# Loading tap 0's weights between the two halves of the samples, and splitting its products at output 254

## The chip, the cores and the metric

The kernel runs on one core of one Trainium2 chip. The metric is the device time of one execution in microseconds (us). An execution is also taken by the hardware profiler; its page, its groups of instructions, its waits, its timeline and its chain of work are the "profile" of this text. Engines: PE multiplies matrices (PEld is its weight load), DVE and ACT work on vectors and read PSUM, POOL is the general engine, SP issues the DMAs.

## The reference

Two convolutions of five taps over time, each followed by gelu and by taking every second output, then a joint network: every time step is added to every one of 8 label vectors, tanh, and a last matrix.

```python
B, T, D, K, U = 2, 4000, 512, 5, 8
h = sum over i of einsum("btc,cd->btd", xp[:, i:i+T], w1[i])   # xp: x padded by 2 on both sides
h = gelu(h)[:, ::2]                                             # 2000 steps
f = sum over i of einsum("btc,cd->btd", hp[:, i:i+T1], w2[i])
f = gelu(f)[:, ::2]                                             # 1000 steps
j = tanh((f @ w_f)[:, :, None, :] + (g @ w_g)[:, None, :, :])
return einsum("btud,dv->btuv", j, w_o)
```

Everything is bf16; the result is 2 x 1000 x 8 x 512.

## The kernel before

Channels lie on the 128 partitions in NK = 4 blocks, time along the free dimension. The kernel is a list of operations (`Plan`, L75 to L345): each names its engine, what it reads and writes and an assumed cost. `schedule` (L171) orders the operations of PE, ACT, DVE and POOL by these costs, except those that are pinned to the written order (`pl.pin`); `emit` puts a semaphore wait in front of an instruction whose input comes from another engine or from a DMA. All loads are pinned, so SP issues them in the order in which the code names them. In PSUM the unit of a wait is one of 8 banks; in SBUF it is a cell of 4 bytes.

**First convolution.** The first batch's outputs 0 to ND - 1 (ND = 444) are computed directly: five taps, each of them four column blocks m, each the sum of four products of 128 x 128 weights with ND columns, 80 products in all (`direct`, L750). Their input is `eo`: the samples, turned so that channels are on the partitions, even samples in eo[0] and odd ones in eo[1]. Taps 0, 4 and 2 read even samples, taps 1 and 3 odd ones (`TAPS` = 0, 4, 2, 1, 3).

The samples come by two plain loads of 512 samples each into xr[0] and xr[1] (`load_xr`, L508; "first" and "second" samples below), are turned on PE by products with the identity (L582) into PSUM, and copied from there into `eo` by DVE (L592) and ACT (L480). One copy takes all four channel blocks of every fourth sample; DVE takes one of the two residues r and ACT the other, so their outputs alternate column by column in `eo`:

```python
lo = 16 + 2 * P * rt + r
o = eo[pp, :, lo:lo + 2 * P - 1:2]
```

Two neighbouring bf16 columns share a cell of 4 bytes, so ACT's copy waits for DVE's.

**Order of the loads.** First samples, second samples, tap 0, then the taps 4, 2, 1 and 3 with transposing loads of x into `xa` between them (L520 to L542). A load of a tap waits until the load three places before it has landed (`came[-3]`). Seven products of zeros (`warm_mm`) run before the samples are there, and two more after the first eight turns.

**The other outputs.** The rest of the first convolution is computed in triples (`Triple`, L635): three neighbouring outputs from nine products, instead of fifteen, on sums and differences of samples (`xa`, `xp`, `row`) and of weights (`w1_t`, `w1_x`). The first batch's outputs behind ND are NF = 184 triples on `xa` and NL = 336 on `xp[1]`; the second batch has two lots of 334. DVE and ACT make the sums of weights (`w1part`, L616; wu, ws, wv, ssum are its intermediate tiles) and of samples (`Triple.step`, L651) while PE works on the direct outputs. The weight work begins with taps 0 and 4 and goes on with tap 2. Each unit (one triple lot and one column block m) takes two banks in turn, from the lists `even` and `odd` (L633). The direct outputs use the banks 4, 6, 0 and 2.

**Behind it** come the second convolution, also in triples, and the joint network: tanh on ACT, the last product in a scheme of seven products instead of eight, whose sums POOL makes, and stores of 128 x 512 tiles.

Of the kernel before, what the change touches and what calls it, by code (L numbers as in the profile page):

```python
# [7 lines left out]
ACT = mybir.ActivationFunctionType  # L8
# [4 lines left out]
P = 128  # L13
# [341 lines left out]
def bass_standalone__seq2seq_rnn_t_joint__speech_kernel(  # L355
# [22 lines left out]
    NK = D // P  # L378
    assert (B, T, D, K, U) == (2, 4000, 512, 5, 8)
    T1, T2 = T // 2, T // 4  # L380
    NT3 = (T2 + 2) // 3
    ND, NF = 444, 184
    NL = 2 * NT3 - ND // 3 - NF
    assert ND % 6 == 0 and NF % 2 == 0 and NL % 2 == 0
    EW = 16 + 4 * P
# [5 lines left out]
    NT = 512  # L391
    NWARM = 7
    TAPS = (0, 4, 2, 1, 3)
    NX = 2

    with ExitStack() as es:
        cur = [16512]

        def at(name, shape, dtype, offset=None):
            o = cur[0] if offset is None else offset  # L400
            b = Buf(nc, name, shape, dtype, o)
            if offset is None:
                cur[0] = (b.end + 31) // 32 * 32
            return b
# [3 lines left out]
        w1_sb = at("w1_sb", [K, NK, D], BF16)  # L408
# [9 lines left out]
        xr = [Buf(nc, f"xr{i}", [4, NK, P], BF16, h_off + 16384 + i * 4096) for i in range(NX)]  # L418
# [10 lines left out]
        ident = at("ident", [P], BF16)  # L429
# [3 lines left out]
        eo = Buf(nc, "eo", [2, NK, EW], BF16, w2_sb.end - w2_sb.bytes)  # L433
# [40 lines left out]
        def tt(eng, o, a, b, op):  # L474
            pl.op(eng, lambda e: e.tensor_tensor(out=o.ap, in0=a.ap, in1=b.ap, op=op), (a, b), (o,),  # L475
                  0.02 + 2.14e-3 * o.ap.free_size() if eng == "pool" else vec_cost(o, (a, b)))

        def act(o, i, func, scale=1.0, bias=None):
            rd = (i,) if bias is None else (i, bias)
            pl.op("act", lambda e: e.activation(o.ap, i.ap, func, scale=scale,  # L480
                                                bias=0.0 if bias is None else bias.ap), rd, (o,),
                  o.ap.free_size() * 0.833e-3 + (0.05 if i.psum else 0.105 if bias is None else 0.186))

        def mm(o, pairs, start, stop, check=True):

            def fn(e):
                for n, (l, r) in enumerate(pairs):
                    ins = e.matmul(o.ap, lhsT=l.ap, rhs=r.ap, start=start and n == 0,  # L488
                                   stop=stop and n == len(pairs) - 1, skip_group_check=not check)
                return ins  # L490
            pl.op("pe", fn, [v for pr in pairs for v in pr], (o,), len(pairs) * max(o.ap.free_size() / 2400 + 0.0028, 0.056))
# [7 lines left out]
            out=idv.ap, in_=zero[0:P].ap, compare_op=ALU.not_equal, fill=1.0, base=0,  # L499
# [5 lines left out]
        def load_w(eng, dst, src, slack=0.0):  # L505
            return pl.dma(eng, lambda e: e.dma_start(dst.ap, src), (), (dst,), slack=slack)

        def load_xr(rt):  # L508
            dst = xr[rt][:].map(lambda a: a.rearrange("p r k c -> p (r k c)"))
            src = x[0, 4 * P * rt:4 * P * (rt + 1), :].rearrange("(p r) c -> p (r c)", r=4)  # L510
            return pl.dma("sp", lambda e: e.dma_start(dst.ap, src), (), (dst,), rate=370e3)
# [50 lines left out]
        for ph in (4, 0, 2, 1, 3, 5):  # L562
            load_x6(xp[2], 1, ph, 0, 16)

        def warm_mm(lo, hi):
            z, zz = zero[0:P], zero[:]
            for i in range(lo, hi):
                mm(ps.cols((2 * i + 1) % 8 * NT, NT), [(z, zz)], True, True)
                pl.ops[-1].cost = 0.43

        warm_mm(0, NWARM)
        psb = ps.h[:, :].bitcast(BF16)
        for pp in range(2):
            for rt in range(NX):
                for r in range(2):
                    bk = 2 * rt if pp else 4 * rt + 2 * r
                    lo = bk * 1024 + pp * r * 512
                    pv = View(psb[:, lo:lo + 512].rearrange("p (k c) -> p k c", k=NK), np.array([bk]), True)

                    def fn(e, rt=rt, pp=pp, r=r, pv=pv):  # L580
                        for k in range(NK):
                            ins = e.transpose(pv.ap[:, k, :], xr[rt].h[:, 2 * r + pp, k, :], ident.h[:, :])  # L582
                        return ins
                    pl.op("pe", fn, (xr[rt][:], ident[:]), (pv,), 0.22 if pp and rt else 0.43)
                    if not pp and not rt and r:
                        warm_mm(NWARM, NWARM + 2)
                    lo = 16 + 2 * P * rt + r
                    o = eo[pp, :, lo:lo + 2 * P - 1:2]
                    if r:
                        act(o, pv, ACT.Copy)  # L590
                    else:
                        pl.op("dve", lambda e, o=o, pv=pv: e.tensor_copy(out=o.ap, in_=pv.ap), (pv,), (o,), vec_cost(o, (pv,)))  # L592

        def stt(eng, o, a, f, b):
            pl.op(eng, lambda e: e.scalar_tensor_tensor(  # L595
                out=o.ap, in0=a.ap, scalar=f, in1=b.ap, op0=ALU.mult, op1=add), (a, b), (o,),
                  vec_cost(o, (a, b), False))
# [32 lines left out]
                tt("dve", w1_t[1, :, sl], w(1), w(3), add)  # L630
                act(w1_t[0, :, sl], w(1), ACT.Copy, scale=2.0)

        even, odd = [4, 6, 0, 2], [1, 3, 5, 7]  # L633

        class Triple:  # L635

# [38 lines left out]
            def product(self, which, m, bank, start):  # L675
                at_z, i = self.HOME[which]
                w, p = self.w[which]
                n = self.n
                mm(ps.cols(bank * NT, n),
                   [(w[p, k, m * P:(m + 1) * P],  # L680
                     self.z_[i, k, self.off:self.off + n] if at_z else self.r_[i, k, 0:n]) for k in range(NK)],
                   start, True, False)


        class Unit:
# [13 lines left out]
                return ps.cols(self.B * NT, self.t.n)  # L699

            def s1(self):
                self.A = even.pop(0)
# [8 lines left out]
            def s3(self):  # L711
                self.t.product("t1", self.m, self.A, False)
                self.t.product("s1", self.m, self.A, False)
                self.B = odd.pop(0)
                stt("dve", self.pb(), self.pa(), 0.5, self.c)
                tt("dve", self.v, self.pb(), self.s, add)
                self.t.out(1, self.m, self.v)

            def s4(self):
                self.t.product("t0", self.m, self.A, False)  # L720
                self.t.product("s0", self.m, self.A, False)
                self.t.out(0, self.m, self.pa())
                even.append(self.A)

            def s5(self):
                self.t.product("ti", self.m, self.B, False)
                self.t.product("si", self.m, self.B, False)
                self.t.out(2, self.m, self.pb())
                odd.append(self.B)

        def to_h(b, j0, n=NT3):
            def out(r, m, src):
# [26 lines left out]

        pl.pin = False  # L760
        h_edges(0)
        for i in TAPS:
            direct(i)
        for m in range(NK):
            v = ps.cols((4 + 2 * m) % 8 * NT, ND).map(lambda a: a.rearrange("p (q r) -> p r q", r=6))
            act(hT[0][:, m, HOFF:HOFF + ND // 6], v, ACT.Gelu_apprx_tanh)
        for m in range(NK):
            w1part(m, "04")
# [12 lines left out]
                load_w("sp", v[:], src.rearrange("(k c) d -> c k d", c=P))  # L781

        def bank():
            even.append(even.pop(0))
            return even[-1] * NT

        def ge():
            c0 = bank()
# [107 lines left out]
                sems[key] = [nc.alloc_semaphore(f"s_o{len(sems)}"), 0]  # L896
            return sems[key]

        even += odd
        odd = free = even  # L900
        H = NT // 2

        def take():
# [263 lines left out]
```

## Time and profile before

| | us |
|---|---|
| median of 3 runs (lowest, highest) | 255.1 (254.69, 255.27) |
| the profiled execution | 254.9 |
| its span, first to last instruction | 253.1 |
| PE busy, of the span | 246.5 |
| DVE busy, ACT busy | 210.4, 210.6 |
| direct products: first at, first triple product at | 7.76, 23.99 |
| mean granted clock of PE | 1.00 |

The page gives the busy time of each engine and the chain of work that ended last, followed back from the last instruction. A busy engine does not have to be the one that sets the end, so it is read together with busy time by stretch, with the chain in order of time, and with the timeline, in which the brackets at a line's end name the idle time before an instruction and what ended it. Durations of PE in the timeline hold the way through the array, so the distance of one start from the next is the cost of a product in a row of them.

### The profile page before, as it was taken

Reading aid. Unit: us, or ns where it says so; the run is one execution under the profiler, and the core shown is the slowest. Engines: PE = TensorE matmul, PEld = TensorE weight load, DVE = VectorE, ACT = ScalarE, POOL = GpSimd, SP = SyncE. Lnnn points to the kernel's source line nnn. Section 1 sums busy time; section 2 is a strip of 40 time slices with the busy share of each in tenths; the row PEclk is TensorE's granted clock in tenths of the full one; section 3 lists DMA queues with packets and bytes.
Section 4 is the critical chain, followed back from the end, with each engine's and each line's share of the span. In section 5 each row is a group of like instructions: output and inputs, shape, how many; then the busy total and the mean of one; then the engine's idle time right before and its main releaser. Section 6 shows DMA issues by size and latency. Waiting matters only on the chain.

```text
span 253.1 us, 5249 instructions
## 1 busy us (share of the span) xinstructions
PE 246.5 (97%) x1899; PEld 180.1 (71%) x1905; DVE 210.4 (83%) x342; ACT 210.6 (83%) x352; POOL 103.1 (41%) x107
## 2 busy tenths in 40 slices
PE   8799999999999999999999999999999999999994
PEld 3355977666666666667458878877778888787882
DVE  2799999955999999196446799799899999999783
ACT  3497989759958866984699999999999999998762
POOL 1000000000000000001518899698998999998500
PEclk9999999999999999999999999999999999999999
DMA  6999999989000034000001322332344446555646
GB/s 246 281 238 189 202 174 185 136 201 322 3 0 0 3 104 148 0 1 3 0 0 64 104 84 85 130 123 85 105 148 143 138 143 203 166 166 171 205 134 222
DMA packets 55159, 31.99 MB, mean 126 GB/s; under 512 B 32062, under 2 KB 54878, under 8 KB 55134
## 3 DMA queue, kind: packets, MB, share of 16 engines
q1 hardware_dynamic: 54846, 31.47, 46.7%
q8 instruction: 15, 0.25, 0.4%
q10 hardware_dynamic: 288, 0.20, 0.3%
q14 instruction: 10, 0.08, 0.1%
HBM read 7.86 MB, written 16.38 MB: 96 GB/s over the span
## 4 chain that ended last, share of the span: by engine, by line
PE 85%; DVE 8%; DMA 3%; issue 2%; ACT 0%; DVEq 0%
PE acc L488 85%; DMA w_sb<-in_w_dram 2%; DVE wu L595 2%; DVE row L475 2%; DMA xr<-in_x_dram 1%; DVE xa L475 1%; DVE ssum L475 1%; DVE w_t L475 1%; DVE og L475 1%; DVE ws L475 0%; DVE w_x L475 0%; DVE sd L475 0%; DVE wv L475 0%; DVE eo L592 0%; DVE acc L595 0%
## 5 line engine op out<-in xcount | busy, mean ns | idle before, releaser
L475 DVE TENSOR_TENSOR og<-acc,sn 128x512 bf16<-128x512 f32 x84 | 55.6, 683 | 6.4 <-PE acc L488 4.4
L480 ACT ACTIVATE jT<-feT,geT 128x1000 bf16<-128x1000 f32 (+6 forms) x56 | 52.6, 1013 | 0.5 <-DVE feT L802 0.4
L488 PE MATMUL acc<-tw,ss 128*128 128x256 f16 x336 | 46.0, 273 | 0.0
L488 PE MATMUL acc<-row,w_sb 128*128 128x334 bf16 (+2 forms) x224 | 38.9, 296 | 0.0
L488 PEld LDWEIGHTS acc<-tw,ss 128*128 128x128 f16 x336 | 32.6, 98 | 7.7 <-ACT sn L909 0.4
L909 ACT ACTIVATE sn<-acc 128x512 f32<-128x512 f32 x54 | 34.6, 654 | 3.8 <-PE acc L488 3.5
L972 POOL TENSOR_TENSOR ss<-jT 128x512 f16<-128x512 bf16 x23 | 28.8, 1263 | 13.4 <-ACT jT L480 10.8
L488 PE MATMUL acc<-wo_sb,jT 128*128 128x256 bf16 (+1 forms) x187 | 31.5, 292 | 0.3
L488 PEld LDWEIGHTS acc<-row,w_sb 128*128 128x128 bf16 x224 | 21.0, 97 | 8.8 <-DVE sd L475 0.2
L472 POOL MEMSET hT<- 128x8 bf16 (+2 forms) x6 | 0.8, 148 | 63.0 <-ACT hT L480 46.3
L480 ACT ACTIVATE jX<-feT,geT 128x1000 bf16<-128x1000 f32 (+4 forms) x28 | 26.2, 983 | 0.0
L480 ACT ACTIVATE hT<-acc 128x334 bf16<-128x334 f32 (+3 forms) x36 | 15.4, 436 | 10.4 <-PE acc L488 9.9
L595 DVE SCALAR_TENSOR_TENSOR acc<-acc,sd 128x334 f32<-128x334 f32 (+2 forms) x24 | 11.6, 485 | 14.4 <-PE acc L488 14.0
L488 PEld LDWEIGHTS acc<-wo_sb,jT 128*128 128x128 bf16 x192 | 18.7, 98 | 6.2
L910 DVE COPY sn<-acc 128x512 f32<-128x512 f32 x30 | 20.5, 685 | 2.5 <-PE acc L488 2.4
L480 ACT ACTIVATE sd<-acc 128x334 f32<-128x334 f32 (+2 forms) x48 | 20.0, 434 | 2.8 <-PE acc L488 1.9
L475 DVE TENSOR_TENSOR row<-row 128x1336 bf16<-128x1336 bf16 (+2 forms) x24 | 19.1, 798 | 0.0
L972 POOL TENSOR_TENSOR ss<-jX 128x512 f16<-128x512 bf16 x15 | 17.4, 1169 | 1.1 <-ACT jX L480 0.6
L488 PE MATMUL acc<-xp,w_t 128*128 128x334 bf16 (+1 forms) x96 | 17.6, 305 | 0.0
L488 PE MATMUL acc<-hT,w_t 128*128 128x334 bf16 x96 | 17.6, 304 | 0.0
L488 PE MATMUL acc<-xp,w_x 128*128 128x334 bf16 (+1 forms) x96 | 17.1, 305 | 0.0
L488 PE MATMUL acc<-eo,w_sb 128*128 128x444 bf16 x80 | 15.6, 351 | 1.4 <-DMA w_sb<-in_w_dram 1.4
(111 smaller groups left out, 513.3 us busy)
## 6 DMA issues: line engine op xcount, KB each, us to landing
out_dram<-og SPq DMA_DIRECT2D x98, 128.0 KB, 2.0
w_sb<-in_w_dram SPq DMA_DIRECT2D x10, 512.0 KB, 5.3
out_dram<-ost SPq DMA_DIRECT2D x10, 128.0 KB, 1.9
xr<-in_x_dram SPq DMA_DIRECT2D x2, 512.0 KB, 3.8
wf_sb<-in_w_f_dram SPq DMA_DIRECT2D x1, 512.0 KB, 3.7
wg_sb<-in_w_g_dram SPq DMA_DIRECT2D x1, 512.0 KB, 4.8
wo_sb<-in_w_o_dram SPq DMA_DIRECT2D x1, 512.0 KB, 5.6
xp<-in_x_dram SPq DMA_TRANSPOSE x18, 4.8
```

The costliest lines, as they stand in the source:

```text
L472: pl.op("pool", lambda e: e.memset(v.ap, 0.0), (), (v,))
L475: pl.op(eng, lambda e: e.tensor_tensor(out=o.ap, in0=a.ap, in1=b.ap, op=op), (a, b), (o,), 0.02 + 2.14e-3 * o.ap.free_size() if eng == "po ...
L480: pl.op("act", lambda e: e.activation(o.ap, i.ap, func, scale=scale, bias=0.0 if bias is None else bias.ap), rd, (o,), o.ap.free_size() * ...
L488: ins = e.matmul(o.ap, lhsT=l.ap, rhs=r.ap, start=start and n == 0, stop=stop and n == len(pairs) - 1, skip_group_check=not check)
L595: pl.op(eng, lambda e: e.scalar_tensor_tensor(out=o.ap, in0=a.ap, scalar=f, in1=b.ap, op0=ALU.mult, op1=add), (a, b), (o,), vec_cost(o, (a ...
L909: pl.flex({"act": (lambda e: e.activation(o.ap, v.ap, ACT.Copy), 0.05 + n * 0.833e-3), "dve": (lambda e: e.tensor_copy(out=o.ap, in_=v.ap) ...
L910: "dve": (lambda e: e.tensor_copy(out=o.ap, in_=v.ap), 0.065 + n * 1.04e-3)}, (v,), (o,))
L972: fn = lambda e, o=S[i], x=x, y=y, op=op: e.tensor_tensor(out=o.ap, in0=x.ap, in1=y.ap, op=op)
```

## The change

The loads now come in the order first samples, tap 0, second samples; the other taps follow as before, and each still waits for the load three places before it. Tap 0's products are split at output NH = 2 x 128 - 2 = 254: the first part needs the first samples alone. The code pins neither part, but PE's order in the changed kernel is: seven products of zeros; the 16 turns of the first samples (even, then odd); 16 products of 254 columns; the 16 turns of the second samples; 16 products of 214 columns; 64 products of 468 columns for the four other taps; the triples. The two products of zeros between the turns are gone.

A turning step now takes half of the channels (two blocks of four) and both residues; DVE copies the first half and ACT the second, so their outputs no longer share cells. ND becomes 468 and NF 176 (NL stays 336). The direct outputs use the banks 0, 2, 4, 6 and the turns the odd banks; the lists of banks change their names and order.

```diff
-    ND, NF = 444, 184
+    ND, NF = 468, 176
...
-        came = [load_xr(rt) for rt in range(NX)]
+        came = [load_xr(0)]
...
         came.append(load_w1(TAPS[0]))
+        came.append(load_xr(1))
         for i in TAPS[1:3]:
             came.append(load_w1(i, came[-3]))
...
+        def turn(rt, pp, cost):
+            for h in range(2):
+                bk = 4 * (rt ^ pp) + 2 * h + 1
+                pv = View(psb[:, bk * 1024:bk * 1024 + 512].rearrange("p (r k c) -> p r k c", r=2, k=2), np.array([bk]), True)
+
+                def fn(e, pv=pv, h=h):
+                    for k in range(2):
+                        for r in range(2):
+                            ins = e.transpose(pv.ap[:, r, k, :], xr[rt].h[:, 2 * r + pp, 2 * h + k, :], ident.h[:, :])
+                    return ins
+                pl.op("pe", fn, (xr[rt][:], ident[:]), (pv,), cost)
+                lo = 16 + 2 * P * rt
+                o = eo[pp, 2 * h:2 * h + 2, lo:lo + 2 * P].map(lambda a: a.rearrange("p k (c r) -> p k c r", r=2))
+                v = pv.map(lambda a: a.rearrange("p r k c -> p k c r"))
+                if h:
+                    act(o, v, ACT.Copy)
+                else:
+                    pl.op("dve", lambda e, o=o, v=v: e.tensor_copy(out=o.ap, in_=v.ap), (v,), (o,), vec_cost(o, (v,)))
...
-        even, odd = [4, 6, 0, 2], [1, 3, 5, 7]
+        bank_a, bank_b = [1, 3, 5, 7], [0, 2, 4, 6]
...
-        def direct(i):
+        NH = 2 * P - 2
+
+        def direct(i, lo=0, hi=ND):
             for m in range(NK):
-                mm(ps.cols((4 + 2 * m) % 8 * NT, ND),
-                   [(w1_sb[i, k, m * P:(m + 1) * P], eo[i % 2, k, 15 + i // 2:15 + i // 2 + ND]) for k in range(NK)],
-                   i == TAPS[0], i == TAPS[-1], False)
+                mm(ps.cols(2 * m * NT + lo, hi - lo),
+                   [(w1_sb[i, k, m * P:(m + 1) * P], eo[i % 2, k, 15 + i // 2 + lo:15 + i // 2 + hi]) for k in range(NK)],
+                   i == TAPS[0] and lo == 0, i == TAPS[-1], False)
...
-        for i in TAPS:
+        turn(0, 0, 0.43)
+        direct(TAPS[0], 0, NH)
+        turn(0, 1, 0.43)
+        turn(1, 0, 0.22)
+        direct(TAPS[0], NH, ND)
+        turn(1, 1, 0.22)
+        for i in TAPS[1:]:
             direct(i)
```

A copy's source in PSUM is now read across the two residues (neighbouring outputs lie 256 columns apart), and its output in `eo` is dense; before, the source was dense and the output took every second column.

More of the change, by code (lines that the diff above doesn't have):

```diff
@@ L563, in bass_standalone__seq2seq_rnn_t_joint__speech_kernel, with warm_mm @@
             load_x6(xp[2], 1, ph, 0, 16)
-        def warm_mm(lo, hi):
+        def warm_mm(n):
             z, zz = zero[0:P], zero[:]
-            for i in range(lo, hi):
-                mm(ps.cols((2 * i + 1) % 8 * NT, NT), [(z, zz)], True, True)
+            for i in range(n):
+                mm(ps.cols(0, NT), [(z, zz)], True, True)
                 pl.ops[-1].cost = 0.43
-        warm_mm(0, NWARM)
+        warm_mm(NWARM)
         psb = ps.h[:, :].bitcast(BF16)
[L573 to L592, printed above, removed]
@@ L701, in s1 @@
             def s1(self):
-                self.A = even.pop(0)
+                self.A = bank_a.pop(0)
                 self.t.product("t2", self.m, self.A, True)
@@ L713, in s3 @@
                 self.t.product("s1", self.m, self.A, False)
-                self.B = odd.pop(0)
+                self.B = bank_b.pop(0)
                 stt("dve", self.pb(), self.pa(), 0.5, self.c)
@@ L722, in s4 @@
                 self.t.out(0, self.m, self.pa())
-                even.append(self.A)
+                bank_a.append(self.A)
             def s5(self):
@@ L728, in s5 @@
                 self.t.out(2, self.m, self.pb())
-                odd.append(self.B)
+                bank_b.append(self.B)
         def to_h(b, j0, n=NT3):
@@ L761, in bass_standalone__seq2seq_rnn_t_joint__speech_kernel @@
         h_edges(0)
-        for i in TAPS:
+        turn(0, 0, 0.43)
[5 more added lines that the diff above has]
+        for i in TAPS[1:]:
             direct(i)
         for m in range(NK):
-            v = ps.cols((4 + 2 * m) % 8 * NT, ND).map(lambda a: a.rearrange("p (q r) -> p r q", r=6))
+            v = ps.cols(2 * m * NT, ND).map(lambda a: a.rearrange("p (q r) -> p r q", r=6))
             act(hT[0][:, m, HOFF:HOFF + ND // 6], v, ACT.Gelu_apprx_tanh)
@@ L783, in bank @@
         def bank():
-            even.append(even.pop(0))
-            return even[-1] * NT
+            bank_a.append(bank_a.pop(0))
+            return bank_a[-1] * NT
         def ge():
@@ L897, in sem_of @@
             return sems[key]
-        even += odd
-        odd = free = even
+        bank_a += bank_b
+        bank_b = free = bank_a
         H = NT // 2
```

## The prediction

> **What bounds the kernel now.** I read the page first: the busy shares, then the chain that ended last, by engine.
>
> ```profile
> PE 246.5 (97%) x1899; PEld 180.1 (71%) x1905; DVE 210.4 (83%) x342; ACT 210.6 (83%) x352; POOL 103.1 (41%) x107
> ...
> PE 85%; DVE 8%; DMA 3%; issue 2%; ACT 0%; DVEq 0%
> ```
>
> PE leads nearly everywhere, yet 8% of the chain is DVE's and 3% DMA's. Next, busy time by stretch (columns after the stretch and its length: PE, PEld, DVE, ACT, POOL, granted clock, DMA share, GB/s); I set the borders where the work changes.
>
> ```profile
> 4.20:7.80 3.60, 2.17 (x24) 1.73 (x24) 2.06 (x3) 1.48 (x2) 0.00 (x0) 1.00 1.02 349
> 7.80:11.20 3.40, 3.10 (x24) 1.63 (x25) 2.21 (x4) 0.75 (x1) 0.00 (x0) 1.00 1.12 246
> 11.20:24.00 12.80, 12.80 (x73) 6.64 (x70) 12.80 (x26) 10.71 (x19) 0.35 (x3) 1.00 1.13 233
> 24.00:33.50 9.50, 9.33 (x113) 8.71 (x111) 9.50 (x21) 9.50 (x20) 0.18 (x2) 1.00 1.07 186
> 33.50:204.50 171.00, 170.95 (x1297) 124.10 (x1298) 142.77 (x226) 148.27 (x248) 69.88 (x63) 1.00 0.35 93
> ```
>
> From 33.5 to 204.5 us PE never waits, so whatever time it gains or loses earlier is handed to the end unchanged. From 11.2 to 33.5 us DVE is full as well, and ACT in the last third. The chain in order of time (start, us, what) says which of them ends last there:
>
> ```profile
> 4.18 4.79 DMA w_sb<-in_w_dram
> 8.96 0.02 issue
> 8.99 0.69 DVE wu L595
> ...
> 32.00 0.43 DVE w_x L475
> 32.43 0.05 issue
> 32.48 98.84 PE acc L488 x710
> ```
>
> Until 32.4 us it is DVE, which combines the weights and samples of the triples and starts when the second weights land at 8.97. So **an earlier start of PE is worth only what DVE can follow.** Last, PE's and DVE's timelines of the start:
>
> ```profile
> 4.21 1.03 PE L582 MATMUL acc<-ident,xr 128*128 128x128 bf16 x8
> 5.03 0.64 PE L488 MATMUL acc<-zero 128*128 128x512 bf16 x2
> 5.50 0.83 PE L582 MATMUL acc<-ident,xr 128*128 128x128 bf16 x12
> 7.76 0.91 PE L488 MATMUL acc<-eo,w_sb 128*128 128x444 bf16 x4 [1.43 <-DMA w_sb<-in_w_dram]
> ```
>
> ```profile
> 8.99 0.69 DVE L595 SCALAR_TENSOR_TENSOR wu<-w_sb 128x512 f32<-128x512 bf16 x1 [1.73 <-DMA w_sb<-in_w_dram]
> 9.60 0.68 DVE L475 TENSOR_TENSOR ws<-w_sb 128x512 f32<-128x512 bf16 x1
> 10.20 0.72 DVE L592 COPY eo<-acc 128x512 bf16<-128x512 bf16 x1
> 10.92 0.69 DVE L595 SCALAR_TENSOR_TENSOR wu<-w_sb,wu 128x512 f32<-128x512 bf16 x1
> ```
>
> PE waits 1.43 us for tap 0's weights; one turning copy sits among DVE's weight work.
>
> **The change part by part.** *Loads.* The first samples land at 4.16 (0.74 + 3.42), the second at 5.4 (issued 1.2, 4.2 to land), tap 0's weights at 7.5 (1.66 + 5.9, the view of that tile). Put ahead of the second samples, tap 0 saves the 1.27 us that these took behind the first: 6.25. First product 0.25 later, as now (7.76 after 7.52): 6.50. Bounds: 6.1, where ACT's copy of the even samples is out (below), and 7.76 if the loads share the engines instead of queueing. The second samples then land by 7.5, since the same bytes have moved. SP's queue: the load of the third weights (tap 2) waits for the load three places before it, which is now tap 0 (6.25) and no longer the second samples (5.4); it and all behind it on SP, two weight loads and the transposing loads of xa and xp, are issued up to 0.8 us later. PE needs the fourth weights at about 17.5 and they landed at 13.9; the last xa landed at 19.8 and is read, in the changed order, at about 21.8: covered. The third weights are not: now they land at 10.8 (5.45 + 5.4) and DVE takes them at 10.92. Bounds: 10.8, if the loads ahead set it, and 11.6, if the 5.4 us run from the issue. I take 10.8: the second weights, issued at 4.18, landed only at 8.97, and a load behind them waits for that and not for its issue.
>
> *Turning and tap 0.* The sixteen first turns run 4.2 to about 5.6; DVE's copies start at 4.85 and 5.47 (0.62 apart, as 5.93's pair), ACT's at 5.3 and 5.95, no longer each behind DVE's, since the halves are separate channels. Two warm-up products go (0.64 beside the wait for loads): nothing. Sixteen products of 254 columns: fifteen of 444 took 2.81 us (21.18 to 23.99), 187.3 ns each, so 2.4 columns per ns and 2.3 ns more; 254 give 108 ns, together 1.73: 8.23. Sixteen second turns at 56 ns (now 5.50 on): 9.13. DVE copies their first half 0.42 after its start, at 8.65, and again at 9.28, and is free at 9.90; ACT copies at 8.93 to 9.68, so PE waits 0.6 and starts the 214-column half at 9.74: 16 x 92 ns to 11.2. Four taps, 64 x 197.5 ns = 12.64, to 23.84, against 23.99 now: **-0.15**. The copies now read PSUM in another stride; as DVE's read of acc in threes (501 elements in 0.68 us) costs no more than a plain one (512 in 0.68), I keep 0.72. Bounds: 0.62 and, were the read at half rate, 1.25.
>
> *Triples.* 36 groups of four products lose 8 of 184 columns: 144 x 3.3 ns = **-0.48**. Their ten or so DVE steps on xa and row lose 32 elements at half a ns: 0.02 each.
>
> *Waits of PE behind 24 us.* Now 0.25 (for ACT's sd), 0.25 and 0.07 (for DVE), 0.57 in all, from PE's timeline. After: DVE starts the weights at 9.90, not 8.99, but has no copy left among them, so the third weights are taken at 11.1, 0.2 later than now. In the changed order, from 9.90 to the last of the four combinations of taps 0, 4 and 2, stand 14 steps of 0.60, 3 of 0.335 and 10 of 0.44, then itself 0.69: 24.5. Behind it ACT has its scaling (0.52), two evictions (0.2 each), a gelu (0.46), one more eviction, a row<-xp of 1.22 and the eviction that PE awaits (0.36): 27.65. PE gets there at 23.84 + 11 x 0.303 + 0.1 = 27.3: 0.4 of waiting. Going through the rest of the order in the same way leaves 0.1 before it and 0.4 behind it, for DVE: 0.9 in all, **+0.35**. PE has less to do and comes sooner; DVE is as late as before. The same walk through the kernel before starts PE's products between 24 and 45 us within 0.1 us of the trace.
>
> Sum: -0.15 - 0.48 + 0.35 = **-0.3 us** of 253.1. The profiled execution took 254.9 (254.6 then), the runs shown have a median of 255.1 (254.8): I say **254.7**. The runs scatter by 0.6 us; within 0.2% (0.5 us) is about what a measurement of this kernel can't tell from no change.
>
> **The clock.** The change adds waits of PE of 0.9 and 0.6 us and drops warm-up work. Now the clock outlasts the 1.43 us wait: turns before it come every 56 ns, products behind it every 187, and the granted clock is 1.00. Had it fallen, sixteen products would take twice 1.73 and the sum would be +1.4, 256.3; I leave that 0.02. The Trainium skill, "TensorE: Matmul & The Clock Gate", section "What's actually happening", has PE back at half clock after an idle window of about 3.4 us. By that rule 0.9 and 0.6 are too short and the sum stays -0.3; the trace agrees with it for 1.43 us, and for no longer wait.
>
> **Rivals.** (1) *Tap 0 lands without its stragglers*: queued straight behind the first samples at the 1.27 us these loads can take, it is there by 5.7; PE starts at 6.1, bound by ACT's copy; DVE is then held by the third weights at 10.8. The sum becomes about -0.7: 254.2, faster. For it: 1.27 for the second samples of the same size. Against it: the weights' loads take 1.45 or more apart (7.52 to 8.97). On the same point the Trainium skill, "DMA: Bandwidth & Descriptors", section "Why a DMA increments its semaphore by 16 and not by 1", says that the slowest of the engines sets a landing; no view here shows the engines apart. 0.30.
> (2) *The strided copies are slow*: two DVE copies behind the second turns at 1.25 instead of 0.72 move the start of the weights by 1.05, and PE with them: 255.6 to 255.8, slower. It decides from 0.25 us a copy, where the gain is gone. Against it: the reads in threes. 0.11.
> (3) *The order doesn't do what it says*: the loads run side by side and tap 0 still lands at 7.5. Then PE's first half ends 1.26 later than forecast, the turns behind it, DVE's weights too: +0.9, 255.9, slower. Against it: the first samples landed 1.27 before the second, though issued 0.46 apart. 0.06.
> (4) *Third weights at 11.6*: DVE 0.5 late instead of 0.2, the sum about +0.1: 255.1, no change; counted with the forecast.
> Forecast, with (4) and its scatter, 0.51.
>
> **Numbers.** Faster by over 0.2%: 0.30, from (1). Within 0.2%: 0.51. Slower: 0.19, from (2), (3) and the clock. The forecast's own range is 254.3 to 255.2; the 8-in-10 range takes in (1) with the scatter and the middle of (2): 254.0 to 255.7.
>
> **What would show it.** Right: tap 0's first product near 6.5, second turns near 8.2, DVE's first wu near 9.9, PE's first triple product near 23.8, waits of PE of about 0.9 us between 24 and 40, and the product of 334 columns (52.08 now) 0.3 earlier. Wrong: a first product at 6.1 or 7.7; copies over 0.9; a DVE gap ahead of the third weights.

## The result, and the profile after

Both kernels were timed on the same chip, 15 runs each: **254.21 us** (253.88 to 254.98) with the change, 254.91 us (254.69 to 255.46) before it. The ratio is 0.9971, with a 95% interval of 0.9963 to 0.9980: 0.7 us faster. Forecast were 254.7, no measurable change, and for rival 1 (tap 0 lands without its stragglers) 254.2. Ratios are formed from the executions within 1.5% of the fastest of their kernel; one later execution of the changed kernel, of 670.11 us, is left out by that.

The profiled execution took 253.94 us, its span is 252.2 (253.1 before). On the page of the changed kernel, the busy times and the chain by engine:

```profile
PE 246.4 (98%) x1913; PEld 180.9 (72%) x1919; DVE 209.9 (83%) x342; ACT 210.0 (83%) x352; POOL 103.2 (41%) x107
...
PE 87%; DVE 5%; DMA 4%; ACT 1%; issue 1%; SPq 0%; DVEq 0%
```

The busy times have hardly moved: PE does as much as before, within 0.1 us. What went is idle time, 0.8 of the 0.9 us by which the span is shorter. In the chain, DVE's share fell from 8% to 5%. The busy time by stretch, in the columns of the prediction, with the borders where the changed kernel's work changes:

```profile
4.20:7.80 3.60, 3.20 (x36) 2.84 (x36) 1.29 (x2) 1.09 (x2) 0.00 (x0) 1.00 0.96 355
7.80:11.20 3.40, 3.16 (x37) 2.61 (x34) 2.99 (x5) 1.08 (x2) 0.00 (x0) 1.00 1.15 275
11.20:23.11 11.91, 11.91 (x61) 5.86 (x60) 11.91 (x25) 9.98 (x17) 0.35 (x3) 1.00 1.11 225
23.11:37.00 13.89, 13.44 (x152) 11.65 (x151) 13.89 (x29) 12.93 (x28) 0.24 (x2) 1.00 1.08 158
37.00:203.60 166.60, 166.55 (x1259) 120.69 (x1259) 138.73 (x219) 145.00 (x240) 69.86 (x63) 1.00 0.35 94
```

PE is now busy for 3.20 us of the first 3.60, instead of 2.17. But in the fourth stretch, behind the direct outputs, it idles for 0.45 us, and there DVE is full (13.89 of 13.89). The timelines of PE and of DVE at the start of the changed kernel (start, us, what, count, and in brackets the idle time ahead):

```profile
4.21 1.29 PE L583 MATMUL acc<-ident,xr 128*128 128x128 bf16 x16
5.90 1.91 PE L488 MATMUL acc<-eo,w_sb 128*128 128x254 bf16 x16 [0.40 <-ACT eo L480]
7.65 1.05 PE L583 MATMUL acc<-ident,xr 128*128 128x128 bf16 x16
8.94 3.64 PE L488 MATMUL acc<-eo,w_sb 128*128 128x214 bf16 x26 [0.24 <-ACT eo L480]
```

```profile
8.07 1.29 DVE L592 COPY eo<-acc 128x512 bf16<-128x512 bf16 x2 [1.93 <-PE acc L583]
9.28 0.68 DVE L595 SCALAR_TENSOR_TENSOR wu<-w_sb 128x512 f32<-128x512 bf16 x1
9.87 0.69 DVE L475 TENSOR_TENSOR ws<-w_sb 128x512 f32<-128x512 bf16 x1
10.70 0.69 DVE L595 SCALAR_TENSOR_TENSOR wu<-w_sb,wu 128x512 f32<-128x512 bf16 x1
```

The order is the one that the change asks for. Tap 0 landed at 5.65 us (7.5 before), the second samples at 7.47 (5.4 before), the second weights at 8.97, where they landed before, and the third at 10.61 (10.83 before). So PE's first product starts 1.86 us earlier (5.90, 7.76 before), and DVE's first weight step 0.29 later (9.28, 8.99). No copy stands among the weight steps any more, so DVE takes the third weights at 10.70, as soon as they are there; before, at 10.92, behind a copy. The first triple product starts at 23.11, against 23.99. The chain of the changed kernel in order of time (start, us, what):

```profile
1.20 4.46 DMA w_sb<-in_w_dram
...
5.67 4.94 DMA w_sb<-in_w_dram
...
10.70 0.69 DVE wu L595
...
24.06 0.63 ACT w_x L480
24.69 0.17 ACT sd L480
```

It goes from tap 0's landing over the third weights, which wait for that landing, to DVE. DVE and then ACT are last until 27.24 us, as the prediction read it in the kernel before (32.4 there). The first product of 334 columns (the second batch) starts at 51.20 us, 52.08 before: 0.88 earlier, and the span is 0.9 shorter. The sum that the trace gives is -0.88 up to the first triple, -0.48 for the narrower triples, +0.47 for more waiting of PE between them.

This execution had an early clock. PE's first turns come about every 107 ns until the trace's clock record turns full (4.72 us here) and every 56 ns from there on; the rows above give 1.00 for the time ahead of the record too. In a second profiled execution of the same kernel (after_again below) the record turns full only at 6.72, so tap 0's first products, at 212 ns each instead of 108, are slow as well:

```profile
5.90 2.31 PE L488 MATMUL acc<-eo,w_sb 128*128 128x254 bf16 x16
8.04 1.06 PE L583 MATMUL acc<-ident,xr 128*128 128x128 bf16 x16
9.34 2.84 PE L488 MATMUL acc<-eo,w_sb 128*128 128x214 bf16 x22 [0.24 <-ACT eo L480]
```

What follows is 0.39 later there: DVE's first weight step at 9.67, the first triple at 23.50, the second batch at 51.59. The third weights happen to land later too, at 11.01, and DVE takes them at 11.10.

### The profile page after: what moved, and what is told of

The parts are those of the page before. It is cut to its first block, busy times and chain, and to the rows that moved or that the text cites. A ratio compares the mean times of both kernels' runs of the same rounds, so it can differ in the third digit from the quotient of the medians.

```text
span 252.2 us, 5270 instructions
## 1 busy us (share of the span) xinstructions
PE 246.4 (98%) x1913; PEld 180.9 (72%) x1919; DVE 209.9 (83%) x342; ACT 210.0 (83%) x352; POOL 103.2 (41%) x107
## 4 chain that ended last, share of the span: by engine, by line
PE 87%; DVE 5%; DMA 4%; ACT 1%; issue 1%; SPq 0%; DVEq 0%
PE acc L488 87%; DMA w_sb<-in_w_dram 4%; DVE wu L595 1%; DVE row L475 1%; DVE xa L475 1%; DVE ssum L475 1%; DVE w_t L475 1%; DVE og L475 1%; ACT row L480 0%; DVE w_x L475 0%; ACT w_x L480 0%; ACT sd L480 0%; ACT hT L480 0%; SPq L511 0%; ACT ost L480 0%
## 5 line engine op out<-in xcount | busy, mean ns | idle before, releaser
L595 DVE SCALAR_TENSOR_TENSOR acc<-acc,sd 128x334 f32<-128x334 f32 (+2 forms) x24 | 11.6, 483 | 13.8 <-PE acc L488 13.7
L488 PE MATMUL acc<-eo,w_sb 128*128 128x468 bf16 (+2 forms) x96 | 16.2, 328 | 0.6 <-ACT eo L480 0.6
```

Of the source, the lines that this page charges most:

```text
L595: pl.op(eng, lambda e: e.scalar_tensor_tensor(out=o.ap, in0=a.ap, scalar=f, in1=b.ap, op0=ALU.mult, op1=add), (a, b), (o,), vec_cost(o, (a ...
```

## The experiments

Two theories. **A, the loads:** the gain is PE's early start, through tap 0's early weights. **B, the turning:** behind the direct outputs DVE and ACT are last, so an early PE is worth little, and the gain comes from turning in channel halves, which takes waits and copies out of the way. The table has all runs. "First product" is PE's first of tap 0, "first triple" the first triple product, "waits" PE's idle time from there to the first product of 334 columns ("second batch"; gaps of over 0.03 us by the distances of its starts, so more than the idle time of a stretch or a bracket shows; the prediction's 0.57 left out the smallest), "DVE" its first weight step, all from one profiled execution each; these starts scatter with the landings of the loads and with the time at which the clock turns full. The median is that of the timed runs, the ratio that to the kernel before on the same chip; the runs come from several chips, so medians are compared by way of the ratios. An edit can also change the order into which `schedule` puts DVE's steps.

| kernel | median us | ratio [95%] | first product | first triple | waits | second batch | DVE |
|---|---|---|---|---|---|---|---|
| before | 254.91 | 1 | 7.76 | 23.99 | 0.63 | 52.08 | 8.99 |
| changed | 254.21 | 0.9971 [0.9963, 0.9980] | 5.90 | 23.11 | 1.10 | 51.20 | 9.28 |
| old_load_order | 254.03 | 0.9960 [0.9946, 0.9973] | 7.74 | 23.66 | 0.65 | 51.28 | 9.13 |
| old_turning | 254.87 | 1.0000 [0.9990, 1.0009] | 6.44 | 24.41 | 0.51 | 51.91 | 9.86 |
| old_nd | 254.74 | 0.9994 [0.9983, 1.0005] | 5.90 | 22.70 | 1.60 | 51.80 | 9.67 |
| no_split | 256.62 | 1.0047 [1.0027, 1.0067] | 9.31 | 26.74 | 0.22 | 53.98 | 9.65 |
| halves_and_468 | 254.29 | 0.9958 [0.9944, 0.9973] | 7.57 | 23.42 | 1.06 | 51.48 | 9.11 |
| halves_only | 254.49 | 0.9969 [0.9954, 0.9984] | 8.16 | 23.22 | 1.11 | 51.75 | 9.36 |
| nd468_only | 255.71 | 1.0011 [0.9996, 1.0026] | 8.35 | 25.41 | 0.55 | 53.02 | 9.50 |
| no_split_warm | 255.38 | 1.0004 [0.9987, 1.0020] | 9.03 | 24.90 | 0.89 | 52.88 | 9.48 |
| after_again | 254.33 | 0.9971 [0.9961, 0.9982] | 5.90 | 23.50 | 1.08 | 51.59 | 9.67 |
| old_load_again | 253.86 | 0.9959 [0.9947, 0.9971] | 7.21 | 23.12 | 0.96 | 51.08 | 8.60 |
| pool3 | 259.29 | see below | 7.15 | 23.06 | see below | 56.25 | 8.62 |
| pool23 | 254.71 | 0.9990 [0.9978, 1.0003] | 7.80 | 23.71 | 1.23 | 51.97 | 9.16 |

### One part undone: the loads, the turning, the lot sizes, the split

*The old order of the loads*, all else as changed:

```diff
-        came = [load_xr(0)]
+        came = [load_xr(0), load_xr(1)]
...
-        came.append(load_xr(1))
```

> The changed kernel with the loads back in the order first samples, second samples, tap 0; all else stays (split at 254, turning in channel halves, 468 direct outputs). Theory A (PE's early start by the new order of the loads is the gain): tap 0's first product goes back from 5.90 to about 7.75, the first triple product with it, and the time to about 254.9, the kernel before's. Theory B (the end of the start is set by DVE, by when it comes to the weights and how much it has to do; PE's early start is given back as waiting): both halves of the samples are turned by 7, DVE starts the weights at the landing of the second ones, 9.0, instead of 9.28, so the time is that of the changed kernel or up to 0.3 us less, 253.9 to 254.3, with less waiting of PE behind 23 us (about 0.5 instead of 1.0).

Measured: 254.03 us, ratio 0.9960 [0.9946, 0.9973]. Undoing the loads takes nothing of the gain. The timeline of PE in this kernel, and its chain up to the triples:

```profile
4.15 3.37 PE L582 MATMUL acc<-ident,xr 128*128 128x128 bf16 x32
7.74 5.59 PE L488 MATMUL acc<-eo,w_sb 128*128 128x254 bf16 x43 [0.23 <-DMA w_sb<-in_w_dram]
```

```profile
1.65 6.04 DMA w_sb<-in_w_dram
7.69 0.05 issue
7.74 13.72 PE acc L488 x84
21.46 0.02 issue
21.49 0.04 ACT hT L480
```

All 32 turns are over before tap 0 is there, and PE then runs through its direct products without a stop. It starts 1.84 us later than in the changed kernel, but reaches the first triple only 0.55 later: in the changed kernel the 16 second turns (0.90 at 56 ns) and the wait for their copies stand among tap 0's products, 1.29 us from the first turn (7.65) to the next product (8.94). The 0.55 goes in the triples, where the changed kernel waits 0.45 longer (1.10, 0.65 here). At the second batch the two are 0.08 apart, less than the 0.39 between the two executions of the changed kernel. The chain shows another limit: here PE itself is last until 21.46, then ACT, and DVE not at all.

*The old turning*, the whole of every second column again, all else as changed (banks and order of the turns too):

```diff
-                pv = View(psb[:, bk * 1024:bk * 1024 + 512].rearrange("p (r k c) -> p r k c", r=2, k=2), np.array([bk]), True)
+                pv = View(psb[:, bk * 1024:bk * 1024 + 512].rearrange("p (k c) -> p k c", k=NK), np.array([bk]), True)
...
-                    for k in range(2):
-                        for r in range(2):
-                            ins = e.transpose(pv.ap[:, r, k, :], xr[rt].h[:, 2 * r + pp, 2 * h + k, :], ident.h[:, :])
+                    for k in range(NK):
+                        ins = e.transpose(pv.ap[:, k, :], xr[rt].h[:, 2 * h + pp, k, :], ident.h[:, :])
...
-                lo = 16 + 2 * P * rt
-                o = eo[pp, 2 * h:2 * h + 2, lo:lo + 2 * P].map(lambda a: a.rearrange("p k (c r) -> p k c r", r=2))
-                v = pv.map(lambda a: a.rearrange("p r k c -> p k c r"))
+                lo = 16 + 2 * P * rt + h
+                o = eo[pp, :, lo:lo + 2 * P - 1:2]
+                v = pv
```

> The changed kernel, but a turning step again takes all channels and one residue, so DVE's and ACT's copies share cells of 4 bytes and ACT's waits for DVE's. Theory A: PE's first product moves from 5.90 to about 6.2, the time by +0.1 to +0.3. Theory B: the copies of the second samples end about 0.7 later, DVE's weights start at 9.3 all the same but PE's second half of tap 0 waits for ACT's copy to about 9.7 or later, and the order worked out by the planner changes; +0.4 to +0.7, 254.6 to 254.9.

Measured: 254.87 us, ratio 1.0000 [0.9990, 1.0009]. The whole gain is gone. PE's timeline and ACT's copies of the second samples in this kernel:

```profile
6.44 1.93 PE L488 MATMUL acc<-eo,w_sb 128*128 128x254 bf16 x16 [0.51 <-ACT eo L480]
8.21 1.06 PE L582 MATMUL acc<-ident,xr 128*128 128x128 bf16 x16
10.25 3.04 PE L488 MATMUL acc<-eo,w_sb 128*128 128x214 bf16 x23 [0.99 <-ACT eo L480]
```

```profile
9.46 1.35 ACT L480 ACTIVATE eo<-acc 128x512 bf16<-128x512 bf16 x2 [2.22 <-DVE eo L591]
```

ACT's copies wait for DVE's again (the releaser is DVE's eo), and PE for ACT's: its first product is 0.54 later than in the changed kernel (5.90 in both executions of that), its second part another 0.75 (a wait of 0.99 instead of 0.24). That is the 1.30 by which the first triple is later (24.41, 23.11). The triples' waits give 0.59 of it back (0.51, 1.10), and 0.71 stays at the second batch (51.91, 51.20). The chain of this kernel runs over DVE's and ACT's copies and PE's direct products; DVE's weight work is not in it, so here it is PE that the old turning holds up. The copies themselves differ too. The view of the tile eo (min, median and max ns; starts), of the changed kernel and then of this one:

```profile
L592 DVE COPY eo<-acc x4: 680/686/692, 4.9 to 8.7; 128x512 bf16<-128x512 bf16 x4
L480 ACT ACTIVATE eo<-acc x4: 591/594/597, 5.1 to 8.8; 128x512 bf16<-128x512 bf16 x4
```

```profile
L591 DVE COPY eo<-acc x4: 706/729/731, 4.8 to 9.3; 128x512 bf16<-128x512 bf16 x4
L480 ACT ACTIVATE eo<-acc x4: 737/740/745, 5.6 to 10.1; 128x512 bf16<-128x512 bf16 x4
```

Same size, same banks; only what is dense differs. With a dense output ACT's copy takes 0.15 us less.

*The old lot sizes*, all else as changed:

```diff
-    ND, NF = 468, 176
+    ND, NF = 444, 184
```

> The changed kernel with 444 direct outputs and 184 triples instead of 468 and 176. Theory A: PE's direct work falls by 0.8 us and its triple work rises by 0.48, so the time falls by 0.3 or stays, 253.9 to 254.3. Theory B: PE comes to the triples at 22.3 instead of 23.1 and waits there for DVE, which has about 0.2 us more to do: waits of PE behind 22 us rise from 1.0 to about 1.7, and the time rises by 0.3 to 0.5, to 254.5 to 254.7.

Measured: 254.74 us, ratio 0.9994 [0.9983, 1.0005], slower than the changed kernel. The first triple comes early (22.70), and PE waits 1.60 us behind it: with fewer direct outputs PE is sooner at the triples than DVE and ACT. Its trace belongs beside after_again's, where the clock turns full about as late (second part at 9.34 in both): the first triple is 0.80 earlier (22.70, 23.50), the second batch 0.21 later (51.80, 51.59). How much of the 0.6 us (by the ratios) is the lot sizes is not shown: the planner also begins DVE's weight work in another order here (two ws, then ssum and wv, ahead of the first wu).

*Tap 0 in one piece* behind all turns, the new loads kept:

```diff
-        direct(TAPS[0], 0, NH)
...
-        direct(TAPS[0], NH, ND)
         turn(1, 1, 0.22)
+        direct(TAPS[0])
```

> The changed kernel with the new order of the loads, but tap 0's products in one piece of 468 columns behind all 32 turns, so PE waits for the second samples (7.47). First product at about 8.8, the first triple product at about 24.6. Theory A: 1.3 us later than the changed kernel at 23.1, so +1.0 to +1.5. Theory B: DVE's copies end at about 9.1 and the weights start as now, PE's waiting behind 23 us falls from 1.0 to 0.3 and gives half of it back: +0.6 to +0.8, 254.8 to 255.0.

Measured: 256.62 us, ratio 1.0047 [1.0027, 1.0067]. PE's timeline shows a longer wait, for the second samples; the busy time by stretch (the granted clock is the third number from the end of a row) shows more than a wait:

```profile
8.02 1.05 PE L583 MATMUL acc<-ident,xr 128*128 128x128 bf16 x16 [2.06 <-DMA xr<-in_x_dram]
9.31 3.92 PE L488 MATMUL acc<-eo,w_sb 128*128 128x468 bf16 x11 [0.24 <-ACT eo L480]
```

```profile
4.00:9.30 5.30, 3.01 (x33) 2.54 (x32) 2.24 (x4) 1.83 (x4) 0.00 (x0) 0.98 0.99 322
9.30:12.70 3.40, 3.38 (x10) 1.34 (x11) 3.40 (x7) 0.98 (x2) 0.00 (x0) 0.52 1.20 290
12.70:17.00 4.30, 4.30 (x23) 2.12 (x22) 4.30 (x9) 4.30 (x9) 0.00 (x0) 1.00 1.19 275
```

In the second row the clock is at about half (0.52), and ten products took the time of nearly twenty. So this kernel tells nothing yet about the split alone.

### One part alone, and the clock

*The turning in halves alone*: the loads, the lot sizes and tap 0 in one piece as before; all 32 turns, with their new banks, stand ahead of tap 0, and the two products of zeros between the turns stay out. Then *the same with 468 and 176*. Against the changed kernel (halves_and_468 without the edit of its first two lines):

```diff
-    ND, NF = 468, 176
+    ND, NF = 444, 184
...
-        came = [load_xr(0)]
+        came = [load_xr(0), load_xr(1)]
...
-        came.append(load_xr(1))
...
-        direct(TAPS[0], 0, NH)
...
-        direct(TAPS[0], NH, ND)
         turn(1, 1, 0.22)
+        direct(TAPS[0])
```

> Turning in channel halves alone, on the old order of the loads, tap 0 in one piece, 444 direct outputs and 184 triples. Theory B in its strong form (taking the copies out of DVE's weight work is the whole gain): 254.1 to 254.4. Theory B with two parts (the shift of eight columns from triples to direct outputs takes about 0.2 us off DVE and gives PE work for the time in which it would wait for DVE): 254.5 to 254.8, with about 0.5 us more waiting of PE behind 22 us than with 468. Theory A: 255.0.

> Two parts of the change without the other two: turning in channel halves and 468 direct outputs with 176 triples; the loads in the old order and tap 0 in one piece. Theory B (DVE sets the end of the start; the order of the loads and the split are worth nothing): all copies are done before the second weights land at about 9.0, DVE goes through the weight work without one, and the time is the changed kernel's, 254.0 to 254.3. Theory A (PE's early start by the loads is the gain): 254.7 to 255.0, like the kernel before.

Measured: 254.49 us, 0.9969 [0.9954, 0.9984], and 254.29 us, 0.9958 [0.9944, 0.9973]. **The new turning, with its banks and its place, is worth as much as the whole change.** PE and DVE in halves_only:

```profile
4.15 2.64 PE L582 MATMUL acc<-ident,xr 128*128 128x128 bf16 x32
8.16 5.06 PE L488 MATMUL acc<-eo,w_sb 128*128 128x444 bf16 x26 [1.38 <-DMA w_sb<-in_w_dram]
```

```profile
4.82 2.48 DVE L591 COPY eo<-acc 128x512 bf16<-128x512 bf16 x4 [3.69 <-PE acc L582]
9.36 0.69 DVE L594 SCALAR_TENSOR_TENSOR wu<-w_sb 128x512 f32<-128x512 bf16 x1 [2.06 <-DMA w_sb<-in_w_dram]
```

All 32 turns and all four of DVE's copies fit into PE's wait for tap 0, and end at 6.8 and 7.3. The 80 products then take 15.06 us (8.16 to 23.22), hardly more than 80 x 187.3 ns = 14.98. Before, 16.23 us (7.76 to 23.99) went by: 12 turns (0.67) and 0.58 of waits stood among them. In this profiled execution tap 0's product came 0.40 later than in that of before, and still the first triple came 0.77 earlier.

*468 and 176 alone*, in the kernel before:

```diff
-    ND, NF = 444, 184
+    ND, NF = 468, 176
```

> The kernel before with 468 direct outputs and 176 triples alone. Its direct work grows by 0.8 us, its triples shrink by 0.48. Theory B: PE is at the triples at 24.8 to 24.9 instead of 23.99, DVE's start at 8.99 and its one copy among the weights stay, PE's waiting behind 24 us falls from 0.57 to about 0.4; the time rises by 0.1 to 0.3, to 255.1 to 255.4, so the larger number pays only where PE comes early. A rival, that fewer triple columns are a gain by themselves: 254.5 to 254.7.

Measured: 255.71 us, 1.0011 [0.9996, 1.0026]: no gain. 24 more columns in 80 products of 2.4 columns per ns cost 0.80 us of PE, the triples give 0.48 back. It pays only where PE would wait for the triples anyway: in the new loads with the turning in halves (old_nd, 0.9994, against 0.9971; the intervals are apart), perhaps in the old ones (0.9969 and 0.9958; they overlap).

*No split, with PE kept at work*: nine products of zeros fill the wait for the second samples.

```diff
-        direct(TAPS[0], 0, NH)
         turn(0, 1, 0.43)
+        warm_mm(9)
+        for o in pl.ops[-9:]:
+            o.cost = 0.2
         turn(1, 0, 0.22)
-        direct(TAPS[0], NH, ND)
         turn(1, 1, 0.22)
+        direct(TAPS[0])
```

> The run with the new order of the loads and tap 0 in one piece, with nine products of zeros more, most of them between the first and the second turns, so that PE is busy while it waits for the second samples. If the fall of the clock (granted 0.82 from 4 to 12 us) is what made that run 256.6 instead of about 255: granted clock 1.00 in all stretches, first triple product at about 24.7 instead of 26.7, 254.8 to 255.2. If the wait for the second samples alone costs it: 256 or more, with the first triple product at 26 or later.

Measured: 255.38 us, 1.0004 [0.9987, 1.0020], a little above what was expected without the fall of the clock. The same stretch is at full clock, in a profiled execution that was the slowest of this kernel (256.31 us):

```profile
9.30:12.70 3.40, 3.40 (x19) 1.66 (x18) 2.91 (x6) 0.91 (x3) 0.00 (x0) 1.00 1.26 216
```

Nineteen products where there were ten. no_split's own runs say the same: its two runs with a mean granted clock of 0.998 took 255.22 and 255.24 us, the six at 0.992 to 0.993 took 255.74 to 256.86. So without the fall of the clock this kernel is even with the kernel before, and 1.1 us behind halves_and_468, which differs by the old loads (255.38 and 254.29 on one chip): the split repairs a late start that the new order itself makes (tap 0 in one piece starts at 9.03, with the old order at 7.57).

### Again, and a test of DVE

The changed kernel and old_load_order once more, now beside each other on one chip:

> The changed kernel itself, on the same chip as the next run, so that the order of the loads is compared directly. Both theories: 0.996 to 0.998 of the kernel before.

> The changed kernel with the loads in the old order, beside the changed kernel on one chip. Theory B (the order of the loads is worth nothing): within 0.3 us of the run of the changed kernel, on either side. Theory A, in what is left of it: at least 0.4 us slower than that.

Measured: 254.33 us, 0.9971 [0.9961, 0.9982], and 253.86 us, 0.9959 [0.9947, 0.9971]. Both ratios are as before. By the ratios the old order is ahead by 0.3 us in both comparisons (by 0.5 in the medians of this one), though the intervals overlap each time. It is the fastest version tried, ahead of both kernels. The traces offer a reason: with the old order the half clock of the start falls on turns that wait for tap 0 anyway (old_load_order's record turns full at 7.1 us and its first product comes at 7.74), while the changed kernel can have products there, which cost it 0.39 us in after_again. That this is the whole of the 0.3 is not shown.

Last, whether less work for DVE ahead of the triples would shorten the waits: in old_load_order one difference of weights (w1_x[2]) goes from DVE to POOL, which idles there, for the column block 3 (pool3) or for 2 and 3 (pool23).

```diff
-                tt("dve", w1_x[2, :, sl], w(1), w(3), sub)
+                tt("pool" if m in POOLM else "dve", w1_x[2, :, sl], w(1), w(3), sub)
```

> The run with the old order of the loads, with one of DVE's steps between 20 and 35 us, the difference of taps 1 and 3 for the last column block (0.335 us on DVE), done by POOL instead, which is idle there. Theory B: the end of the start comes up to 0.15 us sooner than in the run before, PE's waiting behind 23 us falls by that. If DVE doesn't set the end: no change. If POOL's work slows DVE's beside it: slower by 0.2 or more.

> The same with two of these steps, those of the last two column blocks, 0.67 us off DVE. Theory B: 0.3 us sooner than with the old order of the loads alone, about 253.7, and PE's waiting behind 23 us about 0.3 us instead of 0.65. If DVE doesn't set the end: no change. If POOL's work slows DVE's beside it: slower by 0.2 or more.

Measured: 259.29 us for pool3 (two runs at 255.24 and 255.60, the ten others from 258.51 to 260.39; its ratio, 1.0081 [1.0042, 1.0121], counts four of the twelve), and 254.71 us, 0.9990 [0.9978, 1.0003], for pool23. Both are slower than old_load_order. POOL's timeline in pool23, the two steps of it in the view of the tile w_x (min, median and max ns; starts), and POOL's timeline in pool3:

```profile
17.01 12.26 POOL L475 TENSOR_TENSOR w_x<-w_sb 128x512 bf16<-128x512 bf16 x2 [15.02 <-DMA w_sb<-in_w_dram]
```

```profile
L475 POOL TENSOR_TENSOR w_x<-w_sb x2: 1600/6150/10701, 17.0 to 27.7; 128x512 bf16<-128x512 bf16 x2
```

```profile
17.57 10.93 POOL L475 TENSOR_TENSOR w_x<-w_sb 128x512 bf16<-128x512 bf16 x1 [15.58 <-DMA w_sb<-in_w_dram]
```

The first step of 128x512 took POOL 10.7 us in pool23 and 10.9 in pool3, the second in pool23 1.6; its steps of that size later in the kernel take 1.2 to 1.3 (the sums ss of the joint network). In pool3 PE waited 3.97 us ahead of 30.3, and the clock fell once more. DVE's steps kept their length beside most of the long step, but around its end two of them grew: in pool23 one ssum took 1.34 us instead of 0.68 and one w_t 0.87 instead of 0.41. So these kernels don't test what they were made for, and whether a freer DVE would help stays open.

## Why the prediction was right or wrong

**Theory A fell, B holds** for the turning: the loads can be undone without loss, the turning can't. That DVE is the last of the engines behind the direct outputs rests on the chain and on the waits of the changed kernel and of old_nd; in old_load_order and old_turning the chain runs over PE and ACT without DVE, and the one test that gave DVE less work was spoilt by POOL.

**The time.** 254.2 lies within the range and is rival 1's figure, but not the forecast's 254.7: the kernel is faster by more than 0.2%, to which the prediction gave 0.30, against 0.51 for no change. The step that failed is the first of the direct part, tap 0's landing: "Put ahead of the second samples, tap 0 saves the 1.27 us that these took behind the first: 6.25." It landed at 5.65. The forecast let tap 0 come as long behind the load ahead of it as before, 2.1 us (7.5 and 5.4); it came 1.49 behind the first samples. The long step went to the second samples, now in third place: 1.82 behind tap 0. So in both orders it is the load in third place that is late, whichever it is: over the fourteen profiled executions the second load lands 1.2 to 1.5 us behind the first, the third 1.5 to 2.7 behind the second. That the second samples would land by 7.5 was right (7.47). From this term come two others: the first product at 5.90 (forecast 6.50), now released by ACT's copy and no longer by the landing, and DVE's first weight step at 9.28 (9.90). DVE takes the third weights at 10.70, 0.2 earlier than before, but at 11.10 in after_again, which is the forecast's figure: this part goes with the landing (10.61 and 11.01). The direct part ended at 23.11 and not 23.84: the first product came 0.60 earlier, the wait for ACT's copy of the second samples was 0.22 shorter (0.15 of it is the copy itself), and the products took 0.09 more. In after_again the direct part ended at 23.50, so about half of what the forecast lacked here is the early clock of the first profiled execution.

**The turning**, costed at nothing with a risk of being slow (rival 2, 0.11), was the second miss, and the larger one for who wants to know the reason: its copies take 686 ns on DVE (720 before) and 594 on ACT (744). The prediction used ACT's freedom from DVE's copies in its own walk, but booked the result under the loads. It never asked what the same turning, with its banks and its place, would do in the old load order, where it is worth 0.8 us.

**Right in part** was the bound ("an earlier start of PE is worth only what DVE can follow"): of 1.84 us of PE's start against the old order 0.08 are left at the second batch, but 1.29 of them went in PE's own second turns and the wait for their copies, and only 0.45 in waits behind the first triple. **Right** were the triples, -0.48; the waits behind 24 us, forecast 0.9, measured 1.1 by the gaps over 0.03 us, with the largest, forecast at 0.4 before 27.65, found as 0.45 before 27.24; and that only the third weights could be late, which they hardly were (taken at 10.70 and 11.10, against 11.6 of rival 4). What stands ahead of that largest wait, in the changed kernel's chain:

```profile
25.76 1.22 ACT row L480
26.98 0.22 ACT sd L480
27.20 0.05 issue
27.24 9.55 PE acc L488 x104
```

Here is ACT's row<-xp of 1.22 us, the step that the prediction named, and PE behind it.

**Rival 1** came in its place and size: PE at 5.90 (6.1), DVE held by the third weights (0.13 us of idle time ahead of 10.70), -0.9 in the trace (-0.7), and -0.6 by the span of after_again (252.5). **Rival 2** went the other way. **Rival 3** fell: the loads do queue. **The clock** did not fall with waits of 0.40 and 0.24, but without the split it fell in six of eight runs, so the edge is nearer than the 0.02 said. What the prediction overlooked is the half clock ahead of it: "the granted clock is 1.00" held only from 5.10 us on in the kernel before.

**Open:** why the landing of tap 0 scatters so (first products from 7.15 to 8.35 with the old order, of the same loads), by which, with the clock of the start, single profiles differ more than the kernels do; and which of the three things in halves_only, the dense copies, the separate banks or the place of the turns, brings how much with the old loads. old_turning shows the copies' share in the new order only.

## What to carry to other kernels

Before an operand is fetched sooner, look for what stands between its arrival and the next bound, and ask of each part of a change what it would do without the others: here the new turning (a layout that lets two engines copy side by side, its banks and its place) earned all, and the reordered loads nothing. Work that must come anyway (turns, copies) belongs into a wait that is there; moved out of it, it stands in the way of the products. If a wait of 2 us is unavoidable, fill it with idle products, since the clock can cost more than the wait.

## What the runs showed of the hardware

- **A wait of 2.06 us halved the clock for 3.41 us.** In no_split the trace's clock record is full from 5.71, half from 9.12, and full again from 12.54 us. Between 5.71 and 9.12 PE worked for about 1.3 us (0.25 of the first turns and 1.05). Pool3's wait of 3.97 us did the same, from 30.53 to 33.94. nd468_only has a wait of the same 2.06 us (before 8.35) and kept its clock: its record turns full at 4.10, and steps of 3.41 us from there divide the wait into 1.2 and 0.8. The Trainium skill, "TensorE: Matmul & The Clock Gate", section "What's actually happening", has the clock halved after at least one idle window of about 3.4 us that runs freely. The length and the free running agree with these traces (the record turns full for the first time at 4.1 to 7.1 us, in each execution elsewhere); the window need not be idle, though: 1.3 us of work in it was not enough in no_split.
- **The start runs at half clock.** Ahead of the record's first full stretch a turn takes 107 ns and a product of 254 columns 212, behind it 56 and 108. How much of the work falls there changes from one execution to the next, by 0.39 us for the changed kernel.
- **ACT and DVE copy faster into dense columns.** 128x512 bf16 from PSUM: 594 ns on ACT and 686 on DVE with a dense output and a strided source, 744 and 720 with every second column in the output and a dense source.
- **POOL beside a full DVE is very slow.** A two-input step of 128x512 bf16 took 10.7 and 10.9 us while DVE was busy (for 12.30 of 12.30 us and 9.90 of 10.90), the next one 1.6, and such steps 1.2 to 1.3 in a later stage; two of DVE's steps doubled, around the end of the long one. By what the two hinder each other these runs do not show.
